# Attention and gated MLP in one kernel: six buffers of terms instead of five, doubled x and reciprocals, a new order of issue, operands 32 bytes apart

## The chip, the cores and the metric

The kernel runs on one core of a Trainium2 chip. The metric is the device time of one execution in microseconds (us). Five engines work side by side: TensorE (PE) multiplies matrices, ScalarE (ACT), VectorE (DVE) and GpSimd (POOL) do elementwise work, and SyncE (SP) issues the transfers. Each engine works through its own list in the order in which the program wrote it, and waits at an instruction whose operand is not ready.

## The reference

```
scores = cap * tanh(scale * (q @ k.T) / cap)          # 8 batches, 12 heads, 448 rows, head width 64
attn   = exp(scores - max(scores))
x      = (attn / (sum(attn) + 1e-9)) @ v               # heads side by side: x is 448 x 768
h      = relu(x @ w_in)                                # w_in 768 x 1024
u, v   = h[..., :512], h[..., 512:]
v_n    = (v - mean(v)) / sqrt(var(v) + 1e-6)           # over the 512 features
v_s    = w_spatial @ v_n + b_spatial                   # over the 448 rows
out    = (u * v_s) @ w_out                             # w_out 512 x 768
```

All inputs and the output are float32.

## The kernel before

The attention of one batch is worked in three quads of four heads; the 24 quads have a running number, `turn`. The rows of k of a head are cut into seven blocks of 64. For one block of a quad TensorE makes the scores of all four heads by four 64x64 matmuls of 448 columns, four heads on four quadrants (L551); ScalarE takes tanh (L555) and exp (L562, on two blocks at a time) into a buffer of terms `tp` of 2 x 896 floats; TensorE multiplies the terms with v (L572). Such a set of four matmuls is called an R task here. Seven blocks need four buffers `tp`, and there are five of them. They come free when PE has multiplied them and DVE has folded them: DVE takes a running sum and maximum over the buffers (L590), transposes (L598) and reduces (L600); ScalarE moves rows of that (L606), DVE forms denominator and reciprocal (L640, L642), and SP sends the reciprocal out (`rd`, L643) and back over all partitions (`rr`, L647). For the first three quads the sums are made by TensorE with ones (L618).

Meanwhile ScalarE has copied the finished product out of PSUM into `xf` (L578, in the text "xev"). When `rr` has landed POOL multiplies `xf` by it (L657, "xmul"), ScalarE casts the result into the upper part of an operand `xg` (L317, "x cast", 448 columns and then 64 more), and DVE subtracts for the lower part (L313, "xl"). An operand so split into two float32r parts enters three matmuls: high by high, high by low, low by high. There is one buffer `xf` and one `rr`: the xev of a quad waits until both casts and both xl of the quad before are done. Six operands `xg` (two of each quad) make the x of a batch.

The MLP of a batch is then, in matmuls over the full 128x128 array: u (72 of 448 columns, L709 to L711), v (66 of 512 columns, L731 to L736), the statistics and norm of v on DVE and POOL (L754 to L762) with its split into `vh` and `vl`, g = the mixing over rows (44 of 448 columns, L800 to L805) and its product with u on DVE (L810), and o (72 of 448 columns, L825 to L827), which ScalarE copies out (L317) and SP writes (L831).

The order on every engine is set by a planner when the program is built. Every task has an engine, an assumed cost in ns and a key (`KEY` plus the position of its quad or MLP chain); the planner runs the list on the assumed costs and at each moment lets a free engine take the ready task of the lowest key whose buffers are free. On TensorE a task of the other kind (`mode` R or N) costs `TURN` more and its key counts `STICK` more, so runs of attention (R) and of MLP matmuls (N) alternate. The order so found is what is issued:

```python
took = min(fit, key=lambda t: (t.key + (self.STICK if t.mode != mode and e == "T" else 0.0), t.seq))
...
"v": (NB * 2 * D, F32, 1), "tp": (2 * PW, F32, 5),
"xf": (PW, F32, 1), "rr": (PW, F32, 1), "st": (64, F32, 2), **MOE_TAGS, "xg": (XW, F32R, 7),
...
b.t = pools[b.tag].tile([128, n], d, name=b.tag)
```

`PW` is 896 floats. A buffer `xg` is 3,840 bytes a partition and `vh`, `vl` are 2,048, so that all of their matmul operands lie at multiples of 64 bytes.

Of the kernel before, what the change touches and what calls it, by code (L numbers as in the profile page):

```python
# [27 lines left out]
def f(ap):  # L28
    return ap.bitcast(F32)
# [13 lines left out]
class Plan:  # L43
# [196 lines left out]
def attn_moe(ctx, tc, bounded, shared, qk, v, qk2, v2, cap, w_in, w_sp, w_out, out):  # L240
    nc = tc.nc
# [84 lines left out]
    def st2(e, n):  # L326
        return {"V": dve, "P": gp}[e](n)
# [70 lines left out]
    def split_cols(key, n0, n1, put, step=512):  # L398
        return [put(key, i, min(i + step, n1)) for i in range(n0, n1, step)]

    wi32, wo32 = w_in.bitcast(U32), w_out.bitcast(U32)
    wi_t, ws_t, wo_t = [], [], []
    for j in range(2):
        for c in range(NP):
            wi_t.append(split_cols((W_KEYS[0] + c * W_KEYS[1], W_KEYS[5] + c * W_KEYS[6])[j], j * FH, (j + 1) * FH, lambda key, i, n, c=c: split_f64(
                key, wi32[c * 128:(c + 1) * 128, 2 * i:2 * n], wi_h[:, c, i:n], wi_l[:, c, i:n], n - i)))
    for c in range(4):
        ws_t.append(split_f32(W_KEYS[2] + c * 0.2, c))
    for c in range(4):
        wo_t.append(split_cols(W_KEYS[3] + c * W_KEYS[4], 0, DM, lambda key, i, n, c=c: split_f64(  # L410
            key, wo32[c * 128:(c + 1) * 128, 2 * i:2 * n], wo_h[:, c, i:n], wo_l[:, c, i:n], n - i, True), WO_N))
# [114 lines left out]
    def quad_bnd(b, n):  # L526

        at, turn = b * H + 4 * n, b * (NP // 2) + n
        kk = lambda name, i=0: at + KEY[name] + KEY.get(name + "_", KEY["step"]) * i
        raw, ready = [], []  # L530
# [77 lines left out]
        d = add("V", 150, kk("dn"), lambda: nc.vector.tensor_tensor(sec(0), st.t[:96, :n1], sh.t[:96, :n1], op=ALU.max), d,  # L608
                [st, sh, dt], [dt], name="mred2")
# [80 lines left out]
    def moe(b, xs):  # L690
        k0 = (b + 1) * H + KEY["moe"]
        step = KEY["span"] / 18.0
        xuse, xdep = [x for x, _ in xs], [d for _, d in xs]
# [24 lines left out]
        def v_part():  # L718


            for t in range(4):
# [28 lines left out]
                else:  # L750
# [159 lines left out]
```

## Time and profile before

| what | value |
|---|---|
| median of 3 runs | 767.34 us (764.82 to 769.64) |
| the profiled execution | 763.54 us |
| its span in the trace | 761.5 us |
| PE busy | 729.1 us, 96% |
| DVE busy | 570.4 us, 75% |
| ACT busy | 483.6 us, 64% |
| POOL busy | 222.9 us, 29% |

The span runs from the first to the last instruction that the profiler saw; about 2.0 us of the profiled execution lie outside of it. The profiled execution is 3.8 us under the median of the three runs.

### The profile page before, as it was taken

The page shows a single profiled execution, that of the slowest core. Times are in us where ns is not written, and L with a number is a line of the kernel's source. Part 1 is how long each engine was busy: PE and PEld are TensorE (multiplying, and loading weights), DVE is VectorE, ACT ScalarE, POOL GpSimd, SP SyncE. Part 2 cuts the span into 40 slices and gives each one's busy share as a digit, 9 for nine tenths or more (in the row PEclk, how much of TensorE's full clock was granted, in tenths as well). Part 3 has the DMA queues.
Part 4 walks back from the last instruction along what each step waited for, and adds up shares of the span by engine and source line. Part 5 has one row for each costly group of instructions (what it writes and reads, how often), then busy time and mean ns, then how long its engine had stood idle before and what let it go on. Part 6 is the DMA issues. An engine that isn't in the chain of part 4 may idle for free. (4 is left out here: it accounts for less than half of the span.)

```text
span 761.5 us, 12261 instructions
## 1 busy us (share of the span) xinstructions
PE 729.1 (96%) x4902; PEld 486.1 (64%) x4902; DVE 570.4 (75%) x713; ACT 483.6 (64%) x648; POOL 222.9 (29%) x181
## 2 busy tenths in 40 slices
PE   8989997899999999999999999999999999999997
PEld 3334565564584765766866756857668658677796
DVE  4988899898986787994886868857877868868230
ACT  6989574757838667676576677377574874672221
POOL 2252253402443024241234013430261212340330
PEclk9999998999999999999999999999999999999999
DMA  7744322433203232214032232042130340101002
GB/s 268 223 149 134 113 88 64 144 109 110 70 5 99 97 97 74 74 61 135 25 97 64 83 122 74 1 122 101 70 98 20 103 145 2 49 25 68 30 1 77
DMA packets 32798, 66.51 MB, mean 87 GB/s; under 512 B 7630, under 2 KB 20444, under 8 KB 32732
## 3 DMA queue, kind: packets, MB, share of 16 engines
q1 hardware_dynamic: 32732, 65.64, 27.1%
q8 instruction: 40, 0.66, 0.4%
q14 instruction: 26, 0.21, 0.1%
HBM read 54.42 MB, written 11.20 MB: 86 GB/s over the span
## 5 line engine op out<-in xcount | busy, mean ns | idle before, releaser
L555 ACT ACTIVATE tp<-ps_s,capt 128x896 f32<-128x896 f32 x168 | 163.8, 1005 | 48.3 <-DVE red L590 26.8
L590 DVE TENSOR_TENSOR red<-red,tp 128x1792 f32<-128x1792 f32 x90 | 146.6, 1628 | 39.4 <-ACT tp L562 37.3
L551 PE MATMUL ps_s<-raw 64*64 64x448 f32 x1344 | 151.5, 545 | 5.8 <-ACT tp L555 5.3
L562 ACT ACTIVATE tp<-tp,capt 128x1792 f32<-128x1792 f32 x96 | 154.2, 1607 | 1.4
L572 PE MATMUL ps_x<-tp,v 64*64 64x448 f32 x1344 | 141.3, 538 | 2.8 <-ACT tp L562 1.6
L657 POOL TENSOR_TENSOR xf<-xf,rr 128x448 f32<-128x448 f32 x48 | 72.1, 1521 | 195.0 <-DMA rr<-rd 155.4
L572 PEld LDWEIGHTS ps_x<-tp,v 64*64 64x64 f32 x1344 | 50.4, 133 | 79.9 <-issue 64.1
L551 PEld LDWEIGHTS ps_s<-raw 64*64 64x64 f32 x1344 | 46.6, 133 | 82.7 <-issue 43.8
L590 DVE TENSOR_TENSOR red<-tp 128x1792 f32<-128x1792 f32 x45 | 91.2, 2026 | 7.2 <-ACT tp L562 5.9
L313 DVE TENSOR_TENSOR xg<-xf,xg 128x448 fp32r<-128x448 f32 x48 | 40.8, 853 | 54.8 <-ACT xg L317 54.5
L313 POOL TENSOR_TENSOR xg<-o,xg 128x448 fp32r<-128x448 f32 x32 | 45.6, 1429 | 107.0 <-ACT xg L317 96.9
L709 PE MATMUL ps_acc<-xg,wi_h 128*128 128x448 f32 x180 | 67.4, 374 | 1.0 <-ACT xg L317 1.0
L825 PE MATMUL ps_acc<-xg,wo_h 128*128 128x448 f32 x176 | 65.5, 372 | 2.3 <-DVE o L810 2.2
L710 PE MATMUL ps_acc<-xg,wi_h 128*128 128x448 f32 x180 | 66.6, 370 | 0.7 <-DVE xg L313 0.7
L711 PE MATMUL ps_acc<-xg,wi_l 128*128 128x448 f32 x180 | 66.5, 369 | 0.0
L826 PE MATMUL ps_acc<-xg,wo_h 128*128 128x448 f32 x176 | 64.5, 366 | 0.0
L827 PE MATMUL ps_acc<-xg,wo_l 128*128 128x448 f32 x176 | 64.4, 366 | 0.0
L758 POOL TENSOR_TENSOR lst<-lst,capt 128x1 f32<-128x1 f32 x32 | 29.8, 935 | 92.2 <-DVE lst L756 92.2
L317 ACT CAST xg<-xf 128x448 fp32r<-128x448 f32 x96 | 35.6, 400 | 26.4 <-POOL xf L657 23.6
L598 DVE STREAM_TRANSPOSE red<-red 128x896 f32<-128x896 f32 x45 | 49.9, 1108 | 1.0
L736 PE MATMUL ps_acc<-wi_h,xg 128*128 128x512 f32 x126 | 49.5, 393 | 1.0 <-DVE xg L313 0.8
L590 DVE TENSOR_TENSOR red<-red 128x896 f32<-128x896 f32 x45 | 49.8, 1107 | 0.6
(141 smaller groups left out, 1192.9 us busy)
## 6 DMA issues: line engine op xcount, KB each, us to landing
raw<-in_qk SPq DMA_DIRECT2D x48, 448.0 KB
v<-in_v SPq DMA_DIRECT2D x24, 448.0 KB
rr<-rd SPq DMA_DIRECT2D x48, 224.0 KB
out<-o SPq DMA_DIRECT2D x48, 224.0 KB
w<-in_w_in SPq DMA_DIRECT2D x12, 512.0 KB
xg<-in_w_out SPq DMA_DIRECT2D x12, 256.0 KB
rd<-dt SPq DMA_DIRECT2D x48, 3.5 KB
wy<-in_w_sp SPq DMA_DIRECT2D x3, 224.0 KB
```

The costliest lines, as they stand in the source:

```text
L313: eng[e].tensor_tensor(o, a, b, op=ALU.subtract)
L551: nc.tensor.matmul(ps.t[c * D:(c + 1) * D, e, :S], lhsT=f(raw[c].t)[r, k:k + D], rhs=f(raw[c].t)[r, :S], start=True, stop=True)
L555: th = add("A", act(PW, 1), kk("th", i), lambda ps=ps, tp=tp, o=o: nc.scalar.activation(out=tp.t[:, o:o + PW].rearrange("p (e q) -> p e q" ...
L562: ex = add("A", act_s(w, 1), kk("ex", i), lambda tp=tp, w=w: nc.scalar.activation(out=tp.t[:, :w], in_=tp.t[:, :w], func=AF.Exp, scale=ca) ...
L572: nc.tensor.matmul(x.t[e * D:(e + 1) * D, c, :S], lhsT=vt.t[c * D:(c + 1) * D, (2 * k + e) * D:(2 * k + e + 1) * D], rhs=tp.t[c * D:(c + 1 ...
L590: nc.vector.tensor_tensor(o_(), i0(), i1(), op=op)
L657: eng[E_X[0]].tensor_tensor(x, x, r, op=ALU.mult)
L709: nc.tensor.matmul(ps, lhsT=wi_h[:, c, fs], rhs=x[:, XH:], start=(c == 0), stop=False)
L710: nc.tensor.matmul(ps, lhsT=wi_h[:, c, fs], rhs=x[:, :S], start=False, stop=False)
L711: nc.tensor.matmul(ps, lhsT=wi_l[:, c, fs], rhs=x[:, XH:], start=False, stop=(c == NP - 1))
L825: nc.tensor.matmul(ps, lhsT=wo_h[:, c, ns], rhs=g[:, XH:], start=(c == 0), stop=False)
L826: nc.tensor.matmul(ps, lhsT=wo_h[:, c, ns], rhs=g[:, :S], start=False, stop=False)
```

## The change

The buffers of terms go from five to six, `xf` and `rr` from one to two each, and the small tiles `lst` of the norm's statistics from 64 floats to 12. The tiles `xg`, `vh` and `vl` are taken 8 floats (32 bytes) longer than they are used, so that the pitch of successive buffers is 3,872 and 2,080 bytes and every second buffer starts 32 bytes off a multiple of 64. The planner's costs, keys and turn penalties are new, and its keys get an addition for each quad or batch from a table. No instruction is added or taken away; what is issued is the same work in another order, with other buffers.

```diff
-    TURN, STICK = 200.0, 1.8364
+    TURN, STICK = 180.0, 2.1477
...
-MM, MMW, TR = 204, 227, 109
-FF = 760
+MM, MMW, TR = 201, 227, 109
+FF = 751
...
-    return 1.04 * n + 70
+    return 1.06 * n + 70
...
-    return 2.17 * n + 120
+    return 2.3 * n + 120
...
+SHIFT = {"xg": 8, "vh": 8, "vl": 8}
...
-    "stg": (512, F32, 2), "o": (448, F32, 2), "lst": (64, F32, 3),
+    "stg": (512, F32, 2), "o": (448, F32, 2), "lst": (12, F32, 3),
...
-    "v": (NB * 2 * D, F32, 1), "tp": (2 * PW, F32, 5),
-    "xf": (PW, F32, 1), "rr": (PW, F32, 1), "st": (64, F32, 2), **MOE_TAGS, "xg": (XW, F32R, 7),
+    "v": (NB * 2 * D, F32, 1), "tp": (2 * PW, F32, 6),
+    "xf": (PW, F32, 2), "rr": (PW, F32, 2), "st": (64, F32, 2), **MOE_TAGS, "xg": (XW, F32R, 7),
...
-BND_KEY = dict(ld=5.4936, vld=3.1608, sc=-1.3285, th=0.5051, ex=-11.3666, pv=2.7084, sm=6.1819, mx=4.2229,
+BND_KEY = dict(ld=14.8556, vld=11.9644, sc=-1.4028, th=3.6395, ex=-2.1311, pv=3.1196, sm=5.8946, mx=3.2381,
...
+BND_ADJ = dict(sc0=0.0171, sc1=-0.118, sc2=0.0775, sc3=0.1227, sc4=0.8882, sc5=1.2454, sc6=-0.1116, sc7=-0.9505,
...
-            b.t = pools[b.tag].tile([128, n], d, name=b.tag)
+            b.t = pools[b.tag].tile([128, n + SHIFT.get(b.tag, 0)], d, name=b.tag)[:, :n]
...
-        kk = lambda name, i=0: at + KEY[name] + KEY.get(name + "_", KEY["step"]) * i
+        own_key = lambda name: KEY[name] + BND_ADJ.get((name if name in ("mx", "sm", "dn", "x") else "sc") + str(turn), 0.0)
+        kk = lambda name, i=0: at + own_key(name) + KEY.get(name + "_", KEY["step"]) * i
...
-            d = [add("A", 220, kk("dn"), lambda p=p, o=o: nc.scalar.copy(out=sh.t[p, :n1 * len(done)], in_=st.t[o, :n1 * len(done)]), d,
+            d = [add("A", 145, kk("dn"), lambda p=p, o=o: nc.scalar.copy(out=sh.t[p, :n1 * len(done)], in_=st.t[o, :n1 * len(done)]), d,
...
-        m = add(E_X[0], st2(E_X[0], 448), k, scaled, deps, [xf, rr], name="xmul")
+        m = add(E_X[0], st2(E_X[0], 448) + (200 if bounded else 0), k, scaled, deps, [xf, rr], name="xmul")
```

The whole order changes with these numbers. Three places show how. In the rows, a name is what an instruction writes, the names behind the arrow are what it reads, and the line is that of the respective kernel (after, lines stand 14 to 17 higher: L571 is tanh, L578 exp, L594 xev, L331 the cast and copy helper, L327 the subtraction, L606 the fold, L659 and L663 the transfers `rd` and `rr`, L848 the write of `out`).

The first is ScalarE's list while PE works the attention run behind the o of the sixth batch. The x casts there are those of quad 20, the last of the seventh batch. Before:

```order
L578 COPY xf<-ps_x 128x896
L317 COPY o<-ps_acc 128x448
L555 ACTIVATE tp<-ps_s,capt 128x896 x2
L562 ACTIVATE tp<-tp,capt 128x1792
L555 ACTIVATE tp<-ps_s,capt 128x896 x2
L317 CAST xg<-xf 128x448
L562 ACTIVATE tp<-tp,capt 128x896
L317 CAST xg<-xf 128x64
L317 CAST xg<-xf 128x448
L555 ACTIVATE tp<-ps_s,capt 128x896
L317 CAST xg<-xf 128x64
L562 ACTIVATE tp<-tp,capt 128x1792
```

The same place after:

```order
L331 COPY o<-ps_acc 128x448
L571 ACTIVATE tp<-ps_s,capt 128x896 x2
L578 ACTIVATE tp<-tp,capt 128x1792
L571 ACTIVATE tp<-ps_s,capt 128x896 x2
L578 ACTIVATE tp<-tp,capt 128x896
L571 ACTIVATE tp<-ps_s,capt 128x896 x2
L578 ACTIVATE tp<-tp,capt 128x1792
L331 CAST xg<-xf 128x448 x2
L331 CAST xg<-xf 128x64 x2
L594 COPY xf<-ps_x 128x896
```

The x casts of quad 20 stood between the tanh and exp of the run, and stand behind its last exp now; the xev of that quad, which stood ahead of the run's first tanh, is issued earlier still (ahead of these rows).

The second is VectorE's list ahead of the last two operands x of batch 1 (the two rows that write `xg`), for which the v of that batch waits. `tp` and `red0` here are folds of the quads behind. Before:

```order
L642 RECIPROCAL dt1_171<-dt1_171 96x28
L590 TENSOR_TENSOR red0_165<-red0_165,tp_1617 128x1792
L590 TENSOR_TENSOR red0_165<-red0_165 128x896
L590 TENSOR_TENSOR red0_165<-red0_165,tp_1676 128x896
L598 STREAM_TRANSPOSE red0_165<-red0_165 128x896
L600 TENSOR_REDUCE st_1717<-red0_165 128x28
L313 TENSOR_TENSOR xg_1730<-xf_1664,xg_1730 128x448
L590 TENSOR_TENSOR red0_165<-tp_1474,tp_1580 128x1792
L313 TENSOR_TENSOR xg_1743<-xf_1664,xg_1743 128x448
```

After:

```order
L658 RECIPROCAL dt1_171<-dt1_171 96x28
L606 TENSOR_TENSOR red0_165<-red0_165 128x896
L606 TENSOR_TENSOR red0_165<-red0_165,tp_1650 128x896
L614 STREAM_TRANSPOSE red0_165<-red0_165 128x896
L616 TENSOR_REDUCE st_1747<-red0_165 128x28
L606 TENSOR_TENSOR red0_165<-tp_1443,tp_1501 128x1792
L327 TENSOR_TENSOR xg_1788<-xf_1480,xg_1788 128x448
L606 TENSOR_TENSOR red0_165<-red0_165,tp_1605 128x1792
L327 TENSOR_TENSOR xg_1801<-xf_1480,xg_1801 128x448
```

One more fold of 1,792 columns stands ahead of the last of the two. Counted from the start of the program, PE's list ahead of the first matmul that reads that operand holds 492 of the small attention matmuls before and 532 after, and 278 MLP matmuls in both.

The third is SyncE's list at the end of the MLP of the sixth batch. Before:

```order
L831 DMA out_0<-o_5181 128x448
L831 DMA out_0<-o_5201 128x448
L831 DMA out_0<-o_5221 128x448
L831 DMA out_0<-o_5240 128x448
L643 DMA rd_5263<-dt0_170 32x2x14 x2
L831 DMA out_0<-o_5261 128x448
L647 DMA rr_5289<-rd_5263 64x2x448 x2
L831 DMA out_0<-o_5287 128x448
```

After:

```order
L848 DMA out_0<-o_5183 128x448
L848 DMA out_0<-o_5203 128x448
L848 DMA out_0<-o_5220 128x448
L848 DMA out_0<-o_5238 128x448
L848 DMA out_0<-o_5256 128x448
L848 DMA out_0<-o_5281 128x448
L659 DMA rd_5294<-dt0_170 32x2x14 x2
L663 DMA rr_5318<-rd_5294 64x2x448 x2
```

The reciprocals of the quad stood among the last two writes of `out`, and stand behind all six now.

## Rows read from the trace of the kernel before

**Rows 1.** Two lines of the profile's page: busy time, share of the span and instructions of each engine, and the granted clock of TensorE in 40 slices of the span, in tenths.

```profile
PE 729.1 (96%) x4902; PEld 486.1 (64%) x4902; DVE 570.4 (75%) x713; ACT 483.6 (64%) x648; POOL 222.9 (29%) x181
...
PEclk9999998999999999999999999999999999999999
```

**Rows 2.** The span in five stretches: the stretch, its length, then the busy time and instructions of PE, PEld, DVE, ACT and POOL, the granted clock, the share of the DMA engines and GB/s.

```profile
6.00:84.00 78.00, 71.42 (x672) 30.27 (x672) 62.52 (x84) 71.20 (x82) 27.92 (x27) 0.98 0.62 196
84.00:191.00 107.00, 96.71 (x598) 62.10 (x598) 97.06 (x139) 65.03 (x95) 32.70 (x31) 0.95 0.31 97
191.00:237.00 46.00, 44.50 (x270) 31.85 (x270) 38.18 (x52) 29.46 (x41) 19.16 (x13) 1.00 0.16 47
237.00:691.00 454.00, 447.64 (x3048) 303.86 (x3047) 348.72 (x397) 298.12 (x394) 128.25 (x94) 1.00 0.24 77
691.00:761.50 70.50, 64.02 (x302) 56.38 (x302) 23.11 (x39) 18.32 (x36) 14.64 (x14) 0.98 0.12 41
```

**Rows 3.** The stretch 237 to 691 us once more, for the scores' line L551 alone and then for L572 alone: PE busy and records, PEld, clock, DMA share, GB/s. One R task leaves eight records.

```profile
237.00:691.00 454.00, 95.20 (x856) 29.02 (x856) 1.00 0.24 77
...
237.00:691.00 454.00, 94.33 (x896) 33.48 (x896) 1.00 0.24 77
```

**Rows 4.** PE's timeline at four places: start, length (matmuls overlap, so lengths are longer than the step from start to start), operation. Between the rows of 247.41 and 261.67 there are 69 matmuls of 448 columns, between those of 708.90 and 710.49 six of 512, between those of 747.03 and 749.09 nine of 448.

```profile
247.41 0.36 PE L826 MATMUL ps_acc<-xg,wo_h 128*128 128x448 f32 x1
...
261.67 0.36 PE L827 MATMUL ps_acc<-xg,wo_l 128*128 128x448 f32 x1
261.97 0.61 PE L551 MATMUL ps_s<-raw 64*64 64x448 f32 x4
...
128.57 0.57 PE L805 MATMUL ps_acc<-ws_h,vl 128*128 128x448 f32 x1
128.94 0.57 PE L803 MATMUL ps_acc<-ws_h,vh 128*128 128x448 f32 x1
...
708.90 0.39 PE L731 MATMUL ps_acc<-wi_h,xg 128*128 128x512 f32 x1
...
710.49 0.39 PE L732 MATMUL ps_acc<-wi_l,xg 128*128 128x512 f32 x1
...
747.03 0.37 PE L825 MATMUL ps_acc<-xg,wo_h 128*128 128x448 f32 x1
...
749.09 0.37 PE L826 MATMUL ps_s<-xg,wo_h 128*128 128x448 f32 x1
```

**Rows 5.** The place at 191 us: two rows of PE's timeline and three of DVE's (in brackets the idle time ahead and what ended it), and the first line of DVE's waits between 9.5 and 191 us (in total, times, longest).

```profile
189.90 0.40 PE L735 MATMUL ps_acc<-wi_l,xg 128*128 128x512 f32 x1
191.10 0.49 PE L736 MATMUL ps_acc<-wi_h,xg 128*128 128x512 f32 x1 [0.81 <-DVE xg L313]
...
187.40 1.18 DVE L313 TENSOR_TENSOR xg<-xf,xg 128x448 fp32r<-128x448 f32 x1 [2.63 <-ACT xg L317]
188.50 2.01 DVE L590 TENSOR_TENSOR red<-tp 128x1792 f32<-128x1792 f32 x1
190.43 0.61 DVE L313 TENSOR_TENSOR xg<-xf,xg 128x448 fp32r<-128x448 f32 x1
...
DVE xg L313 <- ACT xg L317: 11.0, 5, 3.1
```

**Rows 6.** PE's timeline in an attention run between 619 and 626 us; x16 are two R tasks, x8 one.

```profile
619.35 1.68 PE L572 MATMUL ps_x<-tp,v 64*64 64x448 f32 x16
620.85 0.93 PE L551 MATMUL ps_s<-raw 64*64 64x448 f32 x8
...
623.10 0.93 PE L551 MATMUL ps_s<-raw 64*64 64x448 f32 x8
624.52 0.98 PE L572 MATMUL ps_x<-tp,v 64*64 64x448 f32 x8 [0.48 <-ACT tp L562]
```

**Rows 7.** ACT's timeline in the same run.

```profile
622.96 0.56 ACT L317 CAST xg<-xf 128x448 fp32r<-128x448 f32 x1 [1.52 <-POOL xf L657]
623.43 1.04 ACT L562 ACTIVATE tp<-tp,capt 128x896 f32<-128x896 f32 x1
```

**Rows 8.** PE's waits between 237 and 691 us: what waited for what, us in total, times, longest.

```profile
PE ps_s L551 <- ACT tp L555: 2.6, 5, 1.0
PE ps_x L572 <- ACT tp L562: 1.6, 3, 0.7
PE ps_acc L801 <- POOL vl L313: 1.1, 1, 1.1
PE ps_acc L803 <- DVE o L810: 0.7, 1, 0.7
```

**Rows 9.** From a reciprocal's way out to its use, in the slowest quad of the stretch: the issue of `rd` on SP's queue, and the first multiplication by `rr` on POOL.

```profile
466.91 0.80 SPq L643 DMA_DIRECT2D rd<-dt  x2
...
476.90 1.39 POOL L657 TENSOR_TENSOR xf<-xf,rr 128x448 f32<-128x448 f32 x1 [1.21 <-DMA rr<-rd]
```

**Rows 10.** The last quad and the last batch: the last exp on ACT, the last x cast on ACT, and two rows of PE's timeline behind it.

```profile
683.78 1.06 ACT L562 ACTIVATE tp<-tp,capt 128x896 f32<-128x896 f32 x1
...
711.86 0.71 ACT L317 CAST xg<-xf 128x448 fp32r<-128x448 f32 x2 [9.07 <-POOL xf L657]
...
712.48 0.50 PE L734 MATMUL ps_s<-wi_h,xg 128*128 128x512 f32 x1 [0.99 <-ACT xg L317]
...
713.68 0.51 PE L736 MATMUL ps_s<-wi_h,xg 128*128 128x512 f32 x1 [0.47 <-DVE xg L313]
```

More of the change, by code (lines that the diff above doesn't have):

```diff
@@ L224 @@
 ANY_W_KEYS = 2, 0.5, 8, 9, 1, 5, 0.5
-BND_KEY = dict(ld=5.4936, vld=3.1608, sc=-1.3285, th=0.5051, ex=-11.3666, pv=2.7084, sm=6.1819, mx=4.2229,
-               dn=-3.1123, ev=-2.761, x=0.3908, moe=3.1883, span=11.4688, step=-1.4887, mv=-6.4694, sc_=0.4497, th_=0.4533,
-               ex_=1.4867, pv_=0.1452, sm_=0.4695, mx_=0.192)
+BND_KEY = dict(ld=14.8556, vld=11.9644, sc=-1.4028, th=3.6395, ex=-2.1311, pv=3.1196, sm=5.8946, mx=3.2381,
+               dn=-8.7848, ev=1.2169, x=0.1298, moe=2.894, span=12.0158, step=-2.8131, mv=-6.6114, sc_=0.5024, th_=0.4245,
+               ex_=0.8466, pv_=0.1295, sm_=-0.9101, mx_=0.7816)
@@ new lines @@
+BND_ADJ = dict(sc0=0.0171, sc1=-0.118, sc2=0.0775, sc3=0.1227, sc4=0.8882, sc5=1.2454, sc6=-0.1116, sc7=-0.9505,
+               sc8=-0.5792, sc9=-0.2727, sc10=0.2589, sc11=-0.1758, sc21=-0.3588, sc22=-0.8969, sc23=-1.7532, mx0=-3.4104,
+               mx1=-0.7992, mx2=-4.1904, mx3=-2.7969, mx4=0.8121, mx5=-0.5673, mx6=2.4491, mx7=-0.9746, mx8=-2.2675, mx9=-1.2276,
+               mx10=0.4098, mx11=-2.5249, mx21=0.2627, mx22=1.4411, mx23=2.5519, sm0=7.9487, sm1=2.6415, sm2=2.2708, sm3=2.0978,
+               sm4=-1.0422, sm5=1.3077, sm6=0.0328, sm7=-2.8275, sm8=-1.9042, sm9=-0.9183, sm10=-1.3106, sm11=0.8319,
+               sm21=-0.9772, sm22=-0.5575, sm23=7.7438, dn0=-0.11, dn1=2.7441, dn2=5.8521, dn3=2.5287, dn4=1.3886, dn5=-2.5987,
+               dn6=-4.198, dn7=-1.1196, dn8=1.7138, dn9=-0.0419, dn10=-2.5853, dn11=2.9218, dn21=2.974, dn22=0.4959, dn23=8.4234,
+               x0=-0.246, x1=-1.1828, x2=-1.9798, x3=0.1819, x4=-0.8423, x5=0.7767, x6=-1.0621, x7=0.5599, x8=1.4762, x9=1.3748,
+               x10=0.634, x11=1.3752, x21=0.1512, x22=0.5829, x23=1.2875, moe0=1.3077, moe1=-0.5398, moe2=0.3085, moe3=0.2878,
+               moe7=2.8741, span0=-2.9984, span1=0.3732, span2=-1.5001, span3=-0.5929, span7=11.2386, mv0=-0.042, mv1=1.0416,
+               mv2=1.7125, mv3=-0.633, mv7=-1.3107, wi0=-1.094, wi1=-3.5592, wi2=-7.9905, wi3=1.1197, wi4=-2.7735, wi5=0.1607,
+               wi6=-0.4749, wi7=-1.2497, wi8=-1.1526, wi9=-0.7817, wi10=1.1857, wi11=1.8376, ws0=-5.3107, ws1=0.3027, ws2=-3.8674,
+               ws3=0.2305, wo0=0.2652, wo1=0.9306, wo2=0.3634, wo3=1.6944)
@@ L228 @@
 BND_V_FIRST = 1
 WARM, WARM_N = 14, 512
-BND_W_KEYS = -2.7398, 0.1694, 9.1917, 11.5403, 0.2432, 14.1795, 0.5216
+BND_W_KEYS = 3.1523, 0.6521, 9.0883, 11.3327, -0.4642, 13.1561, 0.8331
 SPARE = ()
@@ L399, in split_cols @@
         return [put(key, i, min(i + step, n1)) for i in range(n0, n1, step)]
+    adj = lambda name, i: BND_ADJ.get(name + str(i), 0.0) if bounded else 0.0
     wi32, wo32 = w_in.bitcast(U32), w_out.bitcast(U32)
@@ L657, in scaled @@
                 eng[E_X[0]].tensor_tensor(x, x, r, op=ALU.mult)
-            gs.append(halves(at + 2 * c + KEY["x"], scaled, lambda c=c: xf.t[:, c * S:(c + 1) * S], deps, xf, rr))
+            gs.append(halves(at + 2 * c + own_key("x"), scaled, lambda c=c: xf.t[:, c * S:(c + 1) * S], deps, xf, rr))
         return gs
@@ L690, in moe @@
     def moe(b, xs):
-        k0 = (b + 1) * H + KEY["moe"]
-        step = KEY["span"] / 18.0
+        own_key = lambda name: KEY[name] + (BND_ADJ.get(name + str(b), 0.0) if bounded else 0.0)
+        k0 = (b + 1) * H + own_key("moe")
+        step = own_key("span") / 18.0
         xuse, xdep = [x for x, _ in xs], [d for _, d in xs]
@@ L697, in moe @@
         tags = iter(LAST_TAGS if bounded and b == B - 1 else ["acc"] * 18)
-        kv = lambda k: k + KEY["mv"]
+        kv = lambda k: k + own_key("mv")
         def u_part(js):
@@ L757, in v_part @@
                          [ls], name="stat")
-                s2 = add("P", 464, kv(k), lambda ls=ls: nc.gpsimd.tensor_tensor(ls.t[:, 9:10], ls.t[:, 8:9], half, op=ALU.pow), [s1],
+                s2 = add("P", 520, kv(k), lambda ls=ls: nc.gpsimd.tensor_tensor(ls.t[:, 9:10], ls.t[:, 8:9], half, op=ALU.pow), [s1],
                          [ls])
```

14 lines of the change are left out of this document (7 added, 7 removed).

## The prediction

> **What bounds the kernel now.** I read the page first: TensorE is busy for 729.1 of the 761.5 us and no other engine for more than 570 [rows 1]. So the matmuls set the time wherever they don't stop, and the question is in which stretches they stop and for whom. The table by stretches answers it [rows 2]. In 237 to 691 us, the steady part, PE is idle for 6.4 of 454 us. In 6 to 84 it is idle for 6.6 us, and ACT is busy for 71.2 of the 78: the opening is bound by tanh and exp. In 84 to 191 it is idle for 10.3 us, and DVE is busy for 97.1 of the 107: there the folds and splits pace the program. In 191 to 237 it is idle for 1.5 us.
>
> Then I took the paces of undisturbed matmuls. Seventy steps from 247.41 to 261.67 give 14.26/70 = 0.2037 us for 448 columns; ten steps near 748 give 2.06/10 = 0.206; seven steps near 709 give 1.59/7 = 0.227 for 512 columns; and a change from MLP to attention matmuls takes 0.30 instead of 0.204, so 0.10 for a turn [rows 4]. An R task takes (620.85 - 619.35)/2 = 0.75 us [rows 6].
>
> With these the steady part can be summed. It holds (856 + 896)/8 = 219 R tasks [rows 3], and its other 1,296 records [rows 2] are 5 batches of 66 matmuls of 512 columns and 966 of 448; 41 turns stand in it. 219 x 0.751 + 330 x 0.227 + 966 x 0.204 + 41 x 0.10 = 164.5 + 74.9 + 197.1 + 4.1 = 440.6 us. So 13.4 of the 454 us are lost, 6.4 of them visibly. A stop costs more than its idle time shows: from 189.90 to 191.10 are 1.20 us, where 0.227 would do, a loss of 0.97 with 0.81 shown [rows 5]; from 623.10 to 624.52 are 1.42 for one task, a loss of 0.67 with 0.48 shown [rows 6]. I count 0.2 us on top of each.
>
> **The change part by part.** *The opening.* The place that decides is 191.10, where the v of batch 1 waits for the last half of its x, which DVE makes at 190.43, behind a wait of 2.63 us for a cast and a fold of 2.01 us [rows 5]. In the new order DVE has one fold more to do ahead of that half and nothing less, so it comes 2.0 us later if DVE's idle time stays what it is. PE's list ahead of the same matmul has 532 instead of 492 attention matmuls, ten tasks more, 7.5 us of work done earlier. Gain at this gate: 7.5 - 2.0 = 5.5 us. Of the 1.5 us idle in 191 to 237 I take half, 0.7, since the sixth buffer of terms lets ACT run one more pair of blocks ahead. Together -6.2. The ends: DVE waits 11.0 us for casts in 9.5 to 191, in five waits [rows 5]; if all its 9.9 us of idle time in 84 to 191 went too, -5.5 - 9.9 = -15.4; if PE loses again behind the gate what it did earlier, and the fold is paid, +2.0.
>
> *The steady part.* In before ACT's list of an attention run has the x casts of the quad behind between a tanh and an exp. At 622.96 ACT waits there 1.52 us for POOL's multiplication, and the exp behind it starts at 623.43 [rows 7]; PE, which needs that exp, stops at 624.52 for 0.48 us [rows 6]. The new order has no such cast ahead of the run's last exp, and with a second `xf` the xev no longer waits for it. Stops of this kind, in which PE waits for tanh or exp, are eight with 4.2 us [rows 8]: 4.2 + 8 x 0.2 = 5.8 us. In the same list is one for `vl` from POOL, 1.1 us, 1.3 with the addition, which stood behind such a multiplication. I count both as gone, -7.1. What is late next: a run of 15 R tasks lasts 11.3 us, and ACT has six tanh and one exp of 896 columns in it and two exp of 1,792, by the exp of 896 columns [rows 7] at most 7 x 1.04 + 2 x 2.08 = 11.4 us, so it just keeps up. The ends: 0, if each wait comes back at another place, and -13.4.
>
> *The tail.* Behind the last exp (ends 684.84) come folds, reciprocal, `rd`, `rr` and the multiplication; the cast starts 27.0 us later, at 711.86, and PE stops twice for 0.99 and 0.47 us [rows 10], with the additions 1.8 us. In the new order 94 matmuls of 448 and 42 of 512 columns stand behind the last attention run and ahead of the matmul that needs this cast, 94 x 0.204 + 42 x 0.227 = 28.7 us. The chain of 27.0 and 0.4 for the cast fits into that with 1.3 us to spare. So -1.8; the ends are -2.3 (what is lost there in all) and +2, if this quad's chain grows by a third of the slowest quad's way from `rd` to the multiplication, 10.0/3 = 3.3 us [rows 9].
>
> *Turns.* Counted in the two orders, 65 instead of 71: -6 x 0.10 = -0.6.
>
> *Operands 32 bytes apart.* Nothing in the trace shows an operand off a multiple of 64 bytes, so I bound this by rows. With all operands at multiples of 64 the 448-wide matmuls hold one of two paces, 0.2037 and 0.206 [rows 4]. Were half of the 1,504 at either and all came to the lower one: 752 x 2.3 ns = -1.7 us; all at the higher, +1.7. At the lower level of the clock they start 0.37 us apart [rows 4], which is one column a cycle at 1.2 GHz; one column a cycle at 2.4 GHz would be 0.187, 17 ns under the pace now, so -26 us if nothing but columns were left. I take -1.7, because it is the end that the rows have shown to be held.
>
> The pace at full clock is 204 ns, while the Trainium skill, "TensorE: Matmul & The Clock Gate", section "Back-to-back issue gap", gives an isolated matmul 1/2.4 ns for each column plus 2.5, which is 189 ns here. Its page "SBUF — State Buffer", section "Who interferes with whom", gives TensorE two read ports of its own that it shares with no engine; by that rule a shift of 32 bytes buys nothing, and the sum would lose its 1.7 us; no run here shows yet which of the two holds.
>
> *Without a price:* the shorter `lst` and the new assumed costs do nothing on the chip but through the order.
>
> Sum: -6.2 - 7.1 - 1.8 - 0.6 - 1.7 = -17.4. Against the profiled execution, 763.5 - 17.4 = 746.1; that execution lies 3.8 us under the median of the three runs, so against the median 767.3 - 17.4 = 749.9 us.
>
> **The rivals.** *The opening gains nothing.* ACT (71.2 of 78 us) and DVE (97.1 of 107) pace it [rows 2], both have the same work as before, and moving PE's tasks forward only moves where PE waits. For it speaks that DVE has a fold more ahead of the gate; against it that DVE still idles for 9.9 us. Without the 6.2 us: 756 us.
>
> *The waits return elsewhere.* The stops of the steady part are short ones of many kinds; a new order has its own. Then the tail and the turns are left, -2.4, and with a part of the rest the time ends at 762 to 766.
>
> *The spacing speeds up every matmul.* For it speaks that 17 ns of each 448-wide matmul are unexplained by columns; against it that none of the rows shows them tied to where operands lie. If 11 to 17 of them go, 1,504 x 11 = 17 to 26 us come on top of the other terms: 724 to 735 us.
>
> *SP's queue makes it slower.* In before the reciprocals of a quad leave between the last two writes of `out`; in the new order they stand behind all six, at six batch ends. From `rd` to the multiplication took 10.0 us in the slowest quad [rows 9]. The room: the run of 15 tasks behind the last o, 11.3 us, and twelve 512-wide matmuls that don't need the last two halves, 2.7, less the multiplication 1.4 [rows 9], the cast 0.6 [rows 7] and some 2 for copy, issue and signals (an estimate from these rows), so 10.0. What goes beyond costs PE once at each of the six: 10.0 just fits, and the forecast's 749.9 turns into 775 only where the chain takes 14.2 us or more; at 14.5 it is 777. Against it: the slowest chain in the trace has 4 us less.
>
> **How the numbers follow.** The forecast has 0.55, with its own range of 740 to 758 (the opening within half of its term either way, the steady part between 0.5 and 1.3 of its own, the small terms to their ends). The opening without gain has 0.17, the returning waits 0.14, the faster matmuls 0.08, SP's queue 0.06. I predict 749.9 us. The range, 735 to 763, takes in the opening without gain and the better part of the opening's far end, and leaves out most of the returning waits, SP's queue and half of the faster matmuls. A measurement of this kernel can hardly tell a change under 1%, 7.7 us, from none. Under 759.7 us lie the forecast, the opening without gain and the faster matmuls: 0.80. Returning waits are within 1%: 0.14. SP's queue is slower: 0.06.
>
> **What would show it.** Right: the gate of batch 1's v some 5 us earlier against the work done by then; no PE waits for tanh and exp of the kind of [rows 8] beyond one or two; ACT's casts behind the runs' last exp without PE stopping; PE going through the last batch's v without a stop; the step of 448-wide matmuls at 0.203 to 0.204 throughout. Wrong: PE waits for DVE or ACT in 84 to 191 as long as now; new waits of PE's v for the x casts at batch ends, with `rr` late; a step of 0.19, which would be the spacing's doing; or a step of 0.206 and more.

## The result, and the profile after

The changed kernel takes 744.0 us (median of 4 runs, 741.8 to 746.9) against 767.7 for the kernel before: a ratio of 0.970, with a 95% interval of 0.965 to 0.974. The forecast was 749.9 us with a range of 735 to 763. The profiled execution takes 741.8 us, its span is 739.9; before it was 763.5 and 761.5.

Two lines of the page of after, which answer to [rows 1], and its span in stretches, which answers to [rows 2] (columns as there):

```profile
PE 720.8 (97%) x4902; PEld 489.1 (66%) x4902; DVE 581.1 (79%) x713; ACT 482.4 (65%) x648; POOL 217.6 (29%) x181
...
6.00:84.00 78.00, 70.53 (x673) 31.23 (x672) 63.50 (x83) 71.56 (x81) 23.83 (x26) 0.98 0.62 204
84.00:191.00 107.00, 102.47 (x682) 64.13 (x683) 97.36 (x143) 74.48 (x105) 33.12 (x32) 0.98 0.32 101
191.00:236.00 45.00, 45.00 (x260) 34.83 (x258) 41.04 (x54) 24.25 (x36) 24.61 (x16) 1.00 0.17 52
236.00:661.00 425.00, 424.29 (x2930) 292.06 (x2928) 347.85 (x385) 289.35 (x383) 116.19 (x87) 1.00 0.24 77
661.00:739.90 78.90, 73.67 (x356) 65.21 (x348) 30.57 (x44) 21.23 (x42) 19.66 (x18) 0.99 0.14 48
```

In the steady part PE is idle for 0.7 of 425 us, where it was 6.4 of 454. In 84 to 191 us it is idle for 4.5 instead of 10.3 us, works 682 instead of 598 records in the same time, and its mean granted clock is 0.98 instead of 0.95; DVE is as busy there as before. In 6 to 84 nothing is won. PE's waits after, first those between 6 and 236 us (three longest), then all that is left from 236 us on (in total, times, longest); the second answers to [rows 8]:

```profile
PE ps_x L588 <- DMA v<-in_v: 5.7, 3, 3.0
PE ps_s L567 <- ACT tp L571: 2.3, 2, 1.9
PE ps_x L588 <- ACT tp L578: 1.5, 3, 0.6
...
PE ps_s L567 <- ACT tp L571: 0.7, 1, 0.7
```

The run that answers to [rows 6] and [rows 7], ACT's timeline and POOL's: the exp of 896 columns starts on time, and ACT makes the four x casts behind the exp of 1,792, when POOL has long begun.

```profile
603.85 1.04 ACT L578 ACTIVATE tp<-tp,capt 128x896 f32<-128x896 f32 x1
...
606.56 1.80 ACT L578 ACTIVATE tp<-tp,capt 128x1792 f32<-128x1792 f32 x1
608.24 1.40 ACT L331 CAST xg<-xf 128x448 fp32r<-128x448 f32 x4
...
605.18 3.56 POOL L673 TENSOR_TENSOR xf<-xf,rr 128x448 f32<-128x448 f32 x2 [22.78 <-DMA rr<-rd]
```

### The profile page after: what moved, and what is told of

Its sections match the earlier page's. It is cut to its first block, busy times and chain, and to the rows that moved or that the text cites. A ratio compares the mean times of both kernels' runs of the same rounds, so it can differ in the third digit from the quotient of the medians.

```text
span 739.9 us, 12247 instructions
## 1 busy us (share of the span) xinstructions
PE 720.8 (97%) x4902; PEld 489.1 (66%) x4902; DVE 581.1 (79%) x713; ACT 482.4 (65%) x648; POOL 217.6 (29%) x181
## 4 chain that ended last, share of the span: by engine, by line
PE 89%; DMA 4%; ACT 3%; DVE 2%; issue 1%; SPq 0%; POOL 0%; ACTq 0%; DVEq 0%; POOLq 0%
PE ps_s L567 16%; PE ps_x L588 15%; PE ps_acc L726 5%; PE ps_acc L842 5%; PE ps_acc L727 5%; PE ps_acc L728 5%; PE ps_acc L843 5%; PE ps_acc L844 5%; PE ps_acc L751 4%; PE ps_acc L752 4%; PE ps_acc L753 4%; PE ps_acc L820 2%; PE ps_acc L821 2%; PE ps_acc L822 2%; DMA v<-in_v 2%; PE ps_acc L634 2%
## 5 line engine op out<-in xcount | busy, mean ns | idle before, releaser
L606 DVE TENSOR_TENSOR red<-red,tp 128x1792 f32<-128x1792 f32 x90 | 151.8, 1687 | 50.0 <-ACT tp L578 48.0
L571 ACT ACTIVATE tp<-ps_s,capt 128x896 f32<-128x896 f32 x168 | 162.7, 1005 | 30.2 <-PE ps_s L567 18.7
L578 ACT ACTIVATE tp<-tp,capt 128x1792 f32<-128x1792 f32 x96 | 153.7, 1606 | 1.5
L567 PE MATMUL ps_s<-raw 64*64 64x448 f32 x1344 | 148.9, 545 | 4.5 <-ACT tp L571 3.0
L588 PE MATMUL ps_x<-tp,v 64*64 64x448 f32 x1344 | 143.0, 540 | 7.3 <-DMA v<-in_v 5.7
L673 POOL TENSOR_TENSOR xf<-xf,rr 128x448 f32<-128x448 f32 x48 | 78.3, 1651 | 211.6 <-DMA rr<-rd 184.6
L567 PEld LDWEIGHTS ps_s<-raw 64*64 64x64 f32 x1344 | 48.9, 133 | 77.4 <-issue 48.4
L606 DVE TENSOR_TENSOR red<-tp 128x1792 f32<-128x1792 f32 x45 | 90.9, 2020 | 1.5 <-ACT tp L578 0.4
L327 POOL TENSOR_TENSOR xg<-o,xg 128x448 fp32r<-128x448 f32 x32 | 42.4, 1333 | 95.9 <-ACT xg L331 86.7
L327 DVE TENSOR_TENSOR xg<-xf,xg 128x448 fp32r<-128x448 f32 x48 | 34.9, 730 | 36.9 <-ACT xg L331 36.3
L606 DVE TENSOR_TENSOR red<-red 128x896 f32<-128x896 f32 x45 | 55.0, 1223 | 0.8
L331 ACT COPY o<-ps_acc 128x448 f32<-128x448 f32 x44 | 23.4, 531 | 46.5 <-PE ps_acc L844 35.0
L616 DVE TENSOR_REDUCE st<-red 128x28 f32<-128x896 f32 x45 | 48.8, 1084 | 1.4
```

The costliest lines, as they stand in the source:

```text
L567: nc.tensor.matmul(ps.t[c * D:(c + 1) * D, e, :S], lhsT=f(raw[c].t)[r, k:k + D], rhs=f(raw[c].t)[r, :S], start=True, stop=True)
L571: th = add("A", act(PW, 1), kk("th", i), lambda ps=ps, tp=tp, o=o: nc.scalar.activation(out=tp.t[:, o:o + PW].rearrange("p (e q) -> p e q" ...
L578: ex = add("A", act_s(w, 1), kk("ex", i), lambda tp=tp, w=w: nc.scalar.activation(out=tp.t[:, :w], in_=tp.t[:, :w], func=AF.Exp, scale=ca) ...
L588: nc.tensor.matmul(x.t[e * D:(e + 1) * D, c, :S], lhsT=vt.t[c * D:(c + 1) * D, (2 * k + e) * D:(2 * k + e + 1) * D], rhs=tp.t[c * D:(c + 1 ...
L606: nc.vector.tensor_tensor(o_(), i0(), i1(), op=op)
```

## The experiments

The theory to be tested: the gain is the new order, above all the x casts' place on ACT and attention tasks drawn forward in the opening, and the buffers make that order possible. The rivals: the spacing of 32 bytes; the buffers alone; the numbers (keys and costs) alone. Ratios are to the kernel before, measured beside each run (its medians there are 765.4 to 766.6 us), with 95% intervals. In e3, e8, e11 and e12 the tiles `lst` are 12 floats long too, as in the changed kernel.

**The spacing.** Taken out of the changed kernel (`e1_aligned`), and put alone into the kernel before (`e2_spacing_alone`):

```diff
-SHIFT = {"xg": 8, "vh": 8, "vl": 8}
+SHIFT = {}
```

> The changed kernel with the 32 bytes taken out of xg, vh and vl again: the same buffers, the same order on every engine, all operands at multiples of 64 bytes. My theory: the spacing is not where the time went. In the trace of after the 448-wide steps are 0.6 ns shorter than before and the 512-wide ones 4.3 ns longer; if both are the spacing's doing, taking it out gives 528 x 4.3 ns - 1,504 x 0.6 ns = 1.4 us back: 742.6 us, and 512-wide steps of 0.227 again. Rival A, the spacing made the kernel faster: 17 us or more slower than after, 761 us. Rival B, the place of operands does not matter and the longer 512-wide step comes from something else: 744 us, with the step still at 0.232.

> The kernel before with nothing but the 32 bytes added to xg, vh and vl: old buffers, old order. My theory: no gain, 1.4 us slower by the same two steps, 769 us against 767.7, with 512-wide steps of 0.232 where they were 0.227. Rival A (the spacing is the gain): 741 to 750 us. Rival B: 767.7 us and 0.227.

Measured: e1 742.8 us, 0.972 (0.970 to 0.974), which can't be told from after; e2 1.003 (1.0015 to 1.004), 2.1 us slower than before. PE's steps between 512-wide matmuls of the v, first after (eight steps), then e1 (nine), then e2 (nine; there L733 and L736 are the lines of the v):

```profile
613.07 0.39 PE L751 MATMUL ps_acc<-wi_h,xg 128*128 128x512 f32 x1
...
614.93 0.39 PE L753 MATMUL ps_acc<-wi_h,xg 128*128 128x512 f32 x1
```

```profile
613.05 0.39 PE L752 MATMUL ps_acc<-wi_l,xg 128*128 128x512 f32 x1
...
615.09 0.39 PE L752 MATMUL ps_acc<-wi_l,xg 128*128 128x512 f32 x1
```

```profile
712.69 0.40 PE L736 MATMUL ps_x<-wi_l,xg 128*128 128x512 f32 x1
...
714.79 0.39 PE L733 MATMUL ps_acc<-wi_l,xg 128*128 128x512 f32 x1
```

1.86/8 = 0.2325 with the spacing, 2.04/9 = 0.227 without, 2.10/9 = 0.233 with it in the old order. Over all undisturbed steps the 512-wide ones take 227.6 ns before, 227.5 in e1, 231.9 after and 232.3 in e2; the 448-wide ones 203.9, 202.9, 203.3 and 203.4. So the spacing lengthens 528 steps by 4 to 5 ns and does next to nothing for the mean of the 1,504 others: it costs about 2 us, and rivals A and B both fall.

**The buffers alone.** The order of before on every engine, with larger pools to rotate over:

```diff
+MORE = {"tp": 6, "xf": 2, "rr": 2}
...
-pools = {g: pool(g, n) for g, (_, _, n) in TAGS.items() if g not in LATE}
+pools = {g: pool(g, MORE.get(g, n) if bounded else n) for g, (_, _, n) in TAGS.items() if g not in LATE}
```

> The kernel before, its order on every engine kept as it is, with six buffers of terms, two xf and two rr to rotate over. My theory: buffers alone take away ACT's waits for a free buffer (19.3 us for folds and 8.9 us for xf in 237 to 691 us), but the x casts still stand between tanh and exp in ACT's list and wait for POOL there, so PE's stops for tanh and exp stay for the most part: 762 to 767 us. Rival: the buffers are the gain and the order only uses them: 750 us or less, with PE's waits for tanh and exp in the steady part under 1 us in all.

Measured: 763.4 us, 0.997 (0.996 to 0.998), 2 us of the 23. ACT's waits for folds and for `xf` in the steady part no longer appear among its waits, but PE's stops stay, and so does ACT's wait for POOL at the casts (the steady part, PE's two and ACT's one line):

```profile
PE ps_s L552 <- ACT tp L556: 2.5, 5, 0.9
PE ps_x L573 <- ACT tp L563: 1.6, 3, 0.7
...
ACT xg L318 <- POOL xf L658: 7.6, 6, 1.8
```

Even the 2 us need not come from the waits: PE's 448-wide steps take 202.5 ns here, some 1.3 ns less than before, and 1,504 x 1.3 ns are 2.0 us. A buffer that came free earlier helped nobody here while the list put something late ahead of what it would release.

**The casts put back.** The changed kernel with only ACT's list changed, in four runs (`marks[turn + 1, 6]` is the exp of 896 columns, `c` and `t` are the casts of 448 and of 64 columns):

```diff
+MOVE = 11, 14, 17, 20
...
+            at = tasks.index(marks[turn + 1, 6][0])
+            tasks[at + 1:at + 1] = [t0, m1, c1]
+            tasks[at:at] = [m0, c0]
...
```

> The changed kernel with one thing moved: in four attention runs of the steady part (behind quads 11, 14, 17 and 20) ACT's four x casts go back to where they stood before, one ahead of the exp of 896 columns, the others around the tanh behind it. Every other engine's list is the same. My theory: the first multiplication on POOL ends at about 607 us in the run at 597 to 609 us, the exp of 896 columns now starts at 603.85, so it would start some 3.5 us later and PE stops for most of that: 2 to 3.5 us a run, 8 to 14 us in all, 752 to 758 us, with new waits of PE for tanh and exp in these four runs. Rival: with six buffers ACT's place for the casts is free, and the steady part's gain came from elsewhere: at most 1 us slower, 745 us.

Measured: 759.5 us, 0.993 (0.991 to 0.995): 16.7 us more than e1 on the same chip, so more than two thirds of the whole gain are lost again by sixteen casts. In the profiled executions 15.1 us lie in the four runs and the MLP runs behind them, where PE's list is that of after. The run at 610 to 626 us (ACT, POOL, PE), and then two stretches of it as in the table by stretches (the eighth figure is the granted clock):

```profile
619.64 0.56 ACT L333 CAST xg<-xf 128x448 fp32r<-128x448 f32 x1 [2.85 <-POOL xf L676]
620.11 1.04 ACT L580 ACTIVATE tp<-tp,capt 128x896 f32<-128x896 f32 x1
...
618.25 2.67 POOL L676 TENSOR_TENSOR xf<-xf,rr 128x448 f32<-128x448 f32 x2 [23.02 <-DMA rr<-rd]
...
617.76 1.68 PE L591 MATMUL ps_x<-tp,v 64*64 64x448 f32 x16
622.71 0.98 PE L569 MATMUL ps_s<-raw 64*64 64x448 f32 x8 [3.27 <-ACT tp L573]
...
619.40:622.70 3.30, 0.04 (x4) 0.00 (x0) 1.52 (x2) 3.06 (x6) 1.52 (x2) 1.00 0.11 41
624.10:627.50 3.40, 3.40 (x15) 1.43 (x8) 3.33 (x3) 3.37 (x4) 0.00 (x0) 0.50 0.43 128
```

ACT stands 2.85 us for POOL, PE 3.27 us for ACT. In two of the four runs the clock was granted at the lower level for some 3.4 us soon after the stop, which adds to the 8 to 14 us expected. In the order of after, the casts' place alone is shown to bring the stops back. What it costs there is not what moving the casts had won: in these four runs PE stands for 10.2 us in e4, and stood for 2.1 in the kernel before, with its casts between tanh and exp too. After the change POOL begins its multiplication later in each of the four runs, by 0.2 to 5.2 us. In the run with the casts of quad 20 it was 6.0 us behind the run's first matmul, and is 7.8 (PE and POOL before, then PE after; POOL's row of after, 605.18, stands above):

```profile
614.78 1.73 PE L551 MATMUL ps_s<-raw 64*64 64x448 f32 x16
...
620.78 3.47 POOL L657 TENSOR_TENSOR xf<-xf,rr 128x448 f32<-128x448 f32 x2 [25.08 <-DMA rr<-rd]
...
597.36 1.74 PE L567 MATMUL ps_s<-raw 64*64 64x448 f32 x16
```

**The casts put behind the exp in the kernel before.** Would that alone do? `e10_casts_late` moves casts and subtractions in the same four runs of the old order; e11 adds a sixth buffer of terms, e12 two `xf` and two `rr`, each in rotation only (`marks[turn + 2, 1]` is the exp of 1,792 columns):

```diff
...
+            at = tasks.index(marks[turn + 2, 1][0]) + 1
+            at = max(at, tasks.index(m1) + 1)
+            tasks[at:at] = [c0, l0, c1, l1, t0, t1]
```

> The kernel before with its own buffers (five of terms, one xf, one rr), and one thing moved: in the attention runs behind quads 11, 14, 17 and 20 ACT's four x casts go behind the exp of 1,792 columns that follows them, ahead of the xev, and the subtractions of DVE with them. My theory, that the casts' place on ACT makes PE's stops: these runs lose 1.3, 0.1, 1.4 and 1.5 us or so in before, most of which goes, 3 to 4 us in all, 762 us against 765.4. Rival, that the second xf is what makes the room: the xev waits for the casts and the subtractions behind them, PE's next product for the xev, and nothing is won: 765 us or more.

> The kernel with the casts moved behind the exp (the experiment e10, 769.0 us, old order elsewhere), with six buffers of terms in rotation instead of five and nothing else new. In e10 the stops at the casts are gone, but ACT's tanh behind them waits for DVE's folds, that is for a free buffer of terms (27.4 us in eleven waits in 237 to 700 us), and the copies for the v and u of the MLP stand behind those. My theory: the sixth buffer is what makes the late casts cheap; ACT's waits for folds fall under 10 us and the steady part loses 3 to 5 us less than in the kernel before: 761 to 763 us against 766. Rival: the wait for folds is DVE's lateness and only moves: 767 us or more.

> The same with two xf and two rr in rotation and five buffers of terms. My theory: the xev no longer waits for the subtractions (9.0 us in ten waits in e10), but tanh still waits for the folds: 767 to 769 us, little better than e10. Rival, that the second xf is the one that counts: 761 to 763 us.

Measured: 769.0, 768.9 and 767.9 us; 1.004 (1.002 to 1.006), 1.003 (1.000 to 1.005) and 1.001 (0.999 to 1.004). The stops at the casts behind quads 17 and 20 go as expected (in e11 and e12 that behind quad 14 too), but nothing is won; and my theory for e11 fell: there ACT's wait for the folds is gone too, and it did not help. The same place in e10 (ACT, PE) and in e11 (DVE, ACT, PE):

```profile
634.08 1.31 ACT L319 CAST xg<-xf 128x448 fp32r<-128x448 f32 x4
641.18 1.91 ACT L557 ACTIVATE tp<-ps_s,capt 128x896 f32<-128x896 f32 x2 [1.53 <-DVE red L593]
...
650.74 0.47 PE L713 MATMUL ps_acc<-xg,wi_h 128*128 128x448 f32 x1 [0.84 <-ACT stg L755]
```

```profile
646.70 0.51 DVE L767 TENSOR_SCALAR stg<-stg,lst 128x512 f32<-128x512 f32 x1
...
647.24 0.62 ACT L320 CAST vh<-stg 128x512 fp32r<-128x512 f32 x1 [4.40 <-DVE stg L767]
649.27 0.60 ACT L756 ACTIVATE stg<-ps_acc 128x512 f32<-128x512 f32 x1 [0.48 <-POOL vl L316]
...
649.92 0.47 PE L714 MATMUL ps_acc<-xg,wi_h 128*128 128x448 f32 x1 [0.94 <-ACT stg L756]
```

DVE's subtractions come with the casts, its folds behind them, and the norm of the v behind the folds; ACT's cast of the normed v waits for it 4.40 us, the relu that empties PSUM stands behind that cast, and PE's u waits for the relu. The delay passed from ACT to DVE, back to ACT, and to PE. Here the lists of ACT and DVE were changed in four places and nothing else, and the stop moved; that the other lists have to fit the later cast too is argued from this and not shown.

**Numbers alone, and buffers with the old numbers.** Here the planner makes new orders: with 91 turns in e7 and 79 in e8, against 65. The edit is that of e7, which keeps the spacing; e8 puts the new buffers into the kernel before.

```diff
-    "v": (NB * 2 * D, F32, 1), "tp": (2 * PW, F32, 6),
-    "xf": (PW, F32, 2), "rr": (PW, F32, 2), "st": (64, F32, 2), **MOE_TAGS, "xg": (XW, F32R, 7),
+    "v": (NB * 2 * D, F32, 1), "tp": (2 * PW, F32, 5),
+    "xf": (PW, F32, 1), "rr": (PW, F32, 1), "st": (64, F32, 2), **MOE_TAGS, "xg": (XW, F32R, 7),
```

> The changed kernel's keys, costs and spacing with the old five buffers of terms, one xf and one rr; the planner makes another order out of them, with 91 turns instead of 65 and with x casts ahead of the exps again. My theory: the new order is one that the buffers make possible, and the numbers alone give no gain: 26 turns of 0.1 us and stops in the steady part as in before, 765 to 775 us. Rival: the planner's better costs are the gain: 750 us or less.

> The keys and costs of before with the new buffers; the planner makes an order with 79 turns and with casts ahead of the exp of 1,792 columns, but behind the one of 896. My theory: half the steady part's stops and part of the opening go: 755 to 763 us. Rivals: the buffers alone give all once the planner may use them, 745 us; or nothing, 766 us.

Measured: e7 764.4 us, 0.995 (0.993 to 0.998), e8 766.6 us, 0.999 (0.996 to 1.001). Two stretches of each, and the longest wait of PE in e7's opening:

```profile
84.00:191.00 107.00, 90.42 (x554) 59.24 (x558) 87.71 (x133) 62.41 (x91) 32.45 (x30) 0.90 0.27 88
...
237.00:691.00 454.00, 452.86 (x3075) 306.79 (x3074) 364.61 (x406) 305.25 (x400) 137.45 (x96) 1.00 0.24 76
...
PE ps_acc L817 <- DVE vh L333: 7.6, 1, 7.6
```

```profile
84.00:191.00 107.00, 99.95 (x638) 62.55 (x642) 99.38 (x139) 69.96 (x97) 33.48 (x32) 0.94 0.32 101
...
237.00:691.00 454.00, 444.74 (x2990) 303.19 (x2989) 342.83 (x392) 291.24 (x389) 130.12 (x95) 1.00 0.23 74
```

The new numbers with the old buffers leave PE idle for 1.1 of the steady 454 us, so a steady part nearly without stops needs no buffer; they pay with more turns and a worse opening (90.4 us busy, the clock at 0.90). Nor is the casts' place alone what counts there: behind quads 14 and 17 the first cast stands ahead of the exp of 896 columns in e7, as in e4, and PE does not stop; POOL has begun in time there, 0.1 and 1.6 us behind the run's first matmul (quad 14, ACT and POOL; ACT does not wait for POOL):

```profile
455.40 0.57 ACT L331 CAST xg<-xf 128x448 fp32r<-128x448 f32 x1
455.85 1.05 ACT L578 ACTIVATE tp<-tp,capt 128x896 f32<-128x896 f32 x1
...
452.62 3.30 POOL L673 TENSOR_TENSOR xf<-xf,rr 128x448 f32<-128x448 f32 x2 [22.53 <-DMA rr<-rd]
```

In these runs a cast ahead of an exp stopped PE only where the multiplication that it waits for came late. The new buffers with the old numbers help the opening (99.95 us busy against 96.71 [rows 2]) and worsen the steady part (9.3 us idle against 6.4). By the sum in the next section e7 wins 5.7 us in the steady part and 1.9 in the tail against before and loses 6.6 in the opening and 2.0 by turns. Neither half gives more than 0.5%; together they give 3%. What the numbers would give with five buffers if they were searched for anew was not tried.

**The waits for v in the opening.** A second buffer of v in the room of the second `rr`, and v's loads a quad earlier on SP's list. With one `rr` the planner's order comes out the same on every engine, so the second one is not what makes it. `e9_two_v_aligned` takes the spacing out as well.

```diff
+MORE = {"v": 2}
...
+            load, last = vs_[turn][0], vs_[turn - 2][1] if turn > 1 else None
+            tasks.remove(load)
+            at = tasks.index(last if last else vs_[0][0]) + 1
+            tasks[at:at] = [load]
```

> The changed kernel, whose order on every engine stays, but with one rr (of the two, the order never has two in use at once) and a second buffer of v, and with every load of v placed on SP's list right behind the last use of the v two quads earlier. In after PE waits three times for v in the opening, 0.43, 2.35 and 2.97 us; the first cannot go, the others are the single buffer. My theory: 5.3 us of waits and 0.4 behind them go, but ACT, which is busy for 71.6 of the first 78 us, gives half of it back: 3 us faster than after, 741 us. Rival: ACT and DVE pace the opening anyway, and PE waits for tanh instead: 744 us.

> The same with the spacing of 32 bytes taken out as well. If the two add up: 741 us less 1.3 us (after against the same kernel with aligned operands): 739.5 us.

Measured: 745.1 and 743.9 us, 0.974 (0.971 to 0.976) and 0.972 (0.970 to 0.975), neither to be told from after. The waits of PE in e5's opening:

```profile
PE ps_x L591 <- ACT tp L581: 6.2, 5, 3.2
...
PE ps_x L591 <- DMA v<-in_v: 0.6, 1, 0.6
```

The wait for v goes from 5.7 to 0.6 us and that for exp from 1.5 to 6.2: ACT paces the first 84 us, and the rival was right.

**The way of the reciprocals.** Six small writes of 8 rows behind the last write of `out`:

```diff
+AGAIN = 6
...
+                for i in range(AGAIN if q == 5 else 0):
+                    nc.sync.dma_start(out=out[b, q * 128 + 8 * i:q * 128 + 8 * (i + 1), :], in_=o.t[8 * i:8 * (i + 1)])
```

> The changed kernel with six small writes (8 rows each, of what has just been written) behind the last write of out of every batch, so that the reciprocals of the quad behind leave later on SP. My rival of the prediction had 10.0 us of room from rd to the multiplication, where the trace of after shows 6.7. If the six writes delay rd by 2 us or less, nothing moves: 744 us. If they delay it by 5 us, 1.7 us more than the room is left over at each of five or six batch ends, and PE's v waits for the last x casts: 752 to 754 us. Rival: the room is larger than I reckoned, and even 5 us cost nothing.

Measured: 763.9 us, 0.997 (0.995 to 0.999), 20 us slower than after. SP and POOL at the end of the sixth batch, and three of PE's waits from 237 us on:

```profile
612.41 2.01 SPq L852 DMA_DIRECT2D out<-o  x6
614.52 0.80 SPq L660 DMA_DIRECT2D rd<-dt  x2
...
621.18 2.73 POOL L674 TENSOR_TENSOR xf<-xf,rr 128x448 f32<-128x448 f32 x2 [26.41 <-DMA rr<-rd]
...
PE ps_acc L727 <- ACT stg L769: 5.0, 4, 1.5
PE ps_s L752 <- ACT xg L332: 3.2, 1, 3.2
PE ps_acc L752 <- ACT xg L332: 1.3, 2, 1.0
```

The reciprocal here is ready at 610.5, so the multiplication starts 10.7 us behind it, and the MLP run behind loses 1.9 us more than in after; behind quad 17 it is 11.8 and 3.2, behind quad 14 12.7 and 3.9. All three put the room, counted from the ready reciprocal, at 8.6 to 8.8 us, where after uses 6.9 behind quad 14, 8.0 behind 17 and 7.0 behind 20. So the slower rival of the prediction is a real mechanism, and the changed kernel has 0.7 to 1.8 us to spare. The prediction counted its 10.0 us from the issue of `rd`, 0.3 us later in after; so counted the room is some 8.4 us, and it was put 1.6 too high. The rest of the 20 us lies elsewhere: in the profiled execution some 4 us in the opening, 6 in the tail, where PE stops 3.2 us for the cast of the last quad and the clock is at the lower level for 6.8 us from there on, and 4.6 us behind the last matmul, where the last batch's own six writes stand.

## Why the prediction was right

Forecast and measured by the same sum (tasks and matmuls at the paces of before, turns at 0.10), profiled execution against profiled execution; the measured terms take in the longer 512-wide steps. The opening is cut at 237 us before and 236 after, the tail begins with the first MLP matmul behind the last attention run:

| term | forecast | measured |
|---|---|---|
| opening, to 237 | -6.2 | -10.8 |
| steady part | -7.1 | -8.8 |
| tail | -1.8 | -1.6 |
| turns | -0.6 | -0.6 |
| spacing | -1.7 | about +2, within the terms above |
| sum | -17.4 | -21.8 |

*The opening* was under-sized, in the step that let DVE's half of x come 2.0 us later. The same matmul as at 191.10 in [rows 5], and DVE's half ahead of it, after:

```profile
190.29 0.39 PE L753 MATMUL ps_acc<-wi_h,xg 128*128 128x512 f32 x1
...
187.51 0.61 DVE L327 TENSOR_TENSOR xg<-xf,xg 128x448 fp32r<-128x448 f32 x1
```

The half comes 2.9 us earlier, with a fold more ahead of it. DVE's busy time and instructions up to that half, before and after (stretch, length, busy):

```profile
0.00:190.43 190.43, 159.80 (x227) 0.96 0.45 140
...
0.00:187.51 187.51, 158.22 (x228) 0.98 0.45 144
```

The fold was there, one instruction more, but DVE was busy for 1.6 us less in all and idle for 1.3 us less. So its idle time did not stay what it was, and, what counts for more, the same instructions took some 3.6 us less; why is open. PE passes the gate without a wait, 0.8 us earlier and with ten tasks more behind it, so the gate gave 8.3 us where 5.5 were forecast. What the forecast left out altogether is the clock: between 84 and 191 us it rose from 0.95 to 0.98 [rows 2]. With half of full speed as the lower level, that is (0.05 - 0.02) x 107/0.5 = 6.4 us less at it; a 448-wide step takes 0.37 there instead of 0.204 [rows 4], so 45% of that time, 2.9 us, is an estimate of what came back, within the 8.3 us and not on top of them. No run changes the opening's order alone; that the attention tasks drawn forward made this term is argued from the gate and not shown. The rival "the opening gains nothing" was half right: before 84 us nothing was won, and e5 shows why; between 84 and 191 it fell, with DVE as busy as ever.

*The steady part* won what was told, and PE's stops for tanh and exp are gone but for one. That casts which come late on ACT make such stops is shown by e4. How much of the 8.8 us their new place won is not: before, PE stood for only 2.1 us in the four runs that e4 changed, and e10 took the late casts' stops out of the old order and won nothing. What the prediction put on a second `xf` is not shown: e7 has no stops there with one. *The tail* has no stop left in the last v. *The spacing* was wrong in sign: the forecast looked at the 448-wide step alone and at two paces of it, and the cost came in the 512-wide one, of which it said nothing. The Trainium skill's "SBUF — State Buffer", section "Who interferes with whom", speaks of the read ports that engines share or have alone. That a shift buys nothing was the prediction's inference from it; it fits the mean of the 448-wide steps, and the 4 to 5 ns of the 512-wide ones are no part of it. The other terms won some 2 us more than the table shows, since the spacing's cost lies within them; that the spacing missed its forecast by 3.7 us brought the sum nearer to it, which is luck. *The shorter `lst`*, which was said to do nothing but through the order, may do more: see the last section. *The returning waits* came in e8 and in e10 to e12, and not in the change itself.

## What to carry to other kernels

Where PE is at 96%, look in its suppliers' lists for an instruction that waits for a slow chain and has urgent work queued behind it; put back into the changed kernel, sixteen casts cost 16 us. Such a place costs only as much as the chain is late, so look at both. Here buffers helped only together with an order that uses them, and an order on one engine only together with those of the others: buffers alone gave 0.3%, numbers alone 0.5%, both 3%. Price a stop above its idle time, because the clock may fall behind it.

## What the runs showed of the hardware that was not expected

Operand tiles that begin 32 bytes off a multiple of 64 lengthened the steps of 512-wide float32r matmuls, whose stationary operand is the shifted tile, from 227.5 to 232 ns, and left the mean of the 448-wide ones within 1 ns (e1, e2); why is open. Among the 448-wide ones the tile is the moving operand of u and o, and the stationary one of g. The steps of g differ from kernel to kernel: 204.3 ns before and 204.4 in e10, 200.3 to 200.5 in the six kernels with the short `lst` and no spacing (e1, e3, e8, e9, e11, e12), 203.2 after and 204.2 in e2. The program makes the buffers `vh` and `vl` behind those of `lst`, so a shorter `lst` may move where they begin, in e1 too; no run changes `lst` alone, so this is not shown. And in e4 the granted clock was 0.50 for 3.4 us, with PE busy all that time, 1.4 us after PE had stood for 3.3 us; that run and the MLP run behind it lost 5.1 us against after. The clock also fell to 0.50 for 3.4 us some 0.9 us behind a stop of 2.23 us in e8 and 1.2 us behind one of 1.84 us in e10, and did not behind one of 1.87 us in e11.
